# Two branches of one kernel, their steps listed in another order: local attention and a long convolution on one core

## The chip, the core and the metric

The kernel runs on one core of one Trainium2 chip. The core has five engines with a queue each: TensorE (PE in the profile, with its weight loads shown as PEld), VectorE (DVE), ScalarE (ACT), GpSimd (POOL) and SyncE (SP, which here only issues transfers). Sixteen DMA engines move the data. The metric is the time of one execution on the device in microseconds. Smaller is better.

## The reference

Two computations that share nothing stand side by side; their results are concatenated along the last axis. S = 2048 tokens, D = 576 channels, everything in bf16.

```python
def A(x, wqkv, wo):                 # attention in a dilated local window
    q, k, v = split(x @ wqkv)       # 32 heads of 18 channels
    idx  = pos[:, None] - 2 * arange(8)[None, :]       # 8 earlier tokens, every second one
    attn = softmax(where(idx >= 0, q . k[idx] * 18**-0.5, -1e9))
    return (attn @ v[idx]) @ wo

def B(q, k, v, shift_k, ssm_k, ssm_D):                 # long convolution with a gate
    kv = conv4(k, shift_k) * v      # 4 taps along the tokens, channel by channel
    y  = irfft(rfft(kv, 2 * S) * rfft(ssm_k, 2 * S))[:S] + kv * ssm_D
    return q * y

out = concatenate([A(...), B(...)], axis=-1)           # 2048 x 1152
```

The kernel computes the transforms of B as matrix products in two stages, with a trip through DRAM between them, because the second stage needs another split of the data over the partitions.

## The kernel before

Every piece of work is a small Python function, a *step*. One string lists the steps in the order in which they are emitted; a step's arguments stand behind dots. The framework that builds the program then places the instructions of each engine. It starts from this list, and may let instructions of neighbouring steps pass one another, so each engine's final queue is close to the list and not identical to it.

```python
STEP = dict(xt=x_tr, ia=ia_tables, sk=sk_step, qk=qk_step, qt=qk_tail_step, lkv=load_kv, ..., cv=kv_conv,
            sx=x_part, kt=k_tr, kp=k_part, v=v_step, ha=halo, lm=l_mul, lb=l_sum, sa=softmax_a, sb=softmax_b,
            at=at_step, kl=..., xl=..., ks=k_spec, xs=x_spec, gp=g_prod, gi=g_inv, pm=p_mul, ps=p_sum,
            po=p_out, yl=y_load, ys=y_step)
for item in ORDER.split():
    name, *args = item.split(".")
    STEP[name](*map(int, args))
```

What the steps do, and the lines by which the profile names them:

| Step | Work | Engine and line |
|---|---|---|
| xt | transpose x | PE L285, copies DVE L275 and ACT L288 |
| qk, qt | projections of q and k, 512 columns to a matmul | PE L381, L388, copies ACT L382, L390, L391 |
| ia | tables of the inverse transform | PE L401, copies ACT L404 |
| cv | 4 taps and the product with v of B | DVE L446, L451, L452 |
| sx, kp | first stage of the transform of kv and of ssm_k, written to DRAM (Dx, Dk) | PE L417, copies ACT L421, DMA L424 |
| kt | transpose ssm_k | PE L465, copies DVE L275 |
| v, ha | projection of v; the earlier tokens of the next row | PE L368, copies ACT L369; DMA L593 to L596 |
| lm, lb | products q*k, their sums by head | DVE L486, L488; PE L496, L502, copies ACT L505 |
| sa, sb, at | softmax in two parts, transpose of the weights, once for each half (0, 1) | DVE L512 to L517, ACT L518; DVE L524 to L532; PE L540, copies ACT L542 |
| kl, xl, ks, xs | read Dk or Dx back; second stage of the transform | SP L554; PE L549, copies ACT L551; ks also swaps halves by DMA, POOL L560 and L561 |
| gp, gi | product of the spectra; inverse second stage, written to Dy | DVE L568; PE L582, copies ACT L584, DMA L587 |
| pm, ps, po | weights times v; their sum; output projection | DVE L604, L606; PE L618, L626, copies ACT L623, L628; PE L637, copies ACT L639 |
| yl, ys | read Dy and q of B back; last stage, gate, output | SP L647, POOL L648; PE L657, DVE L658 |

The steps of the convolution and the attention compete for buffers. PSUM has two tiles for each of two pools, and nearly all areas in SBUF are handed out to rings of two to four slots. A step that takes a slot waits until the step that held it has ended:

```python
pa = ctx.enter_context(tc.tile_pool(name="pa", bufs=2, space=PS))   # psA: qk, v, lb, ps, po, at
pb = ctx.enter_context(tc.tile_pool(name="pb", bufs=2, space=PS))   # psB: sx, kp, ks, xs, gi, ys
...
tAr = Ring(mc.take(4, D), mc.take(4, D))                 # result of cv, freed by its last sx
prr = Ring(*[mw.take(2, 2, 128, 8) for _ in range(3)])   # products of lm, freed by lb
Kr  = Ring(mk.take(2, 8, HD), mk.take(2, 8, HD))         # spectra of k, freed by the second gp
Xr  = Ring(mx.take(8, HD), mx.take(8, HD))               # spectra of kv, freed by the second gp
Wr  = Ring(mk.take(8, HD), mk.take(8, HD), wx)           # what kl, xl and yl read: three slots
Pp  = Ring(*[mw.take(2, 4, HD) for _ in range(4)])       # products of gp
```

The steps that matter most in the second half:

```python
def k_spec(i):                                        # ks
    Kc = Kr.get(i)
    s2(Wr[("k", i)], i % 4, Kc[:, 0], 1.0 / 2048)     # 8 matmuls L549, 4 copies L551
    Wr.drop(("k", i))
    nc.gpsimd.dma_start(Kc[0:64, 1], Kc[64:128, 0])   # L560
    nc.gpsimd.dma_start(Kc[64:128, 1], Kc[0:64, 0])   # L561

def g_prod(i, hv):                                    # gp
    nc.vector.tensor_tensor(Pp.get((i, hv)), Kr[i][:, :, 4 * hv:4 * hv + 4, :],
                            Xr[i][:, 4 * hv:4 * hv + 4, :]...to_broadcast([128, 2, 4, HD]), ALU.mult)   # L568
    if hv:
        Kr.drop(i)
        Xr.drop(i)

def at_step(hf):                                      # at: needs sb of the same half
    L = Lh[hf].rearrange("p w (a b) -> p w b a", b=2)
    ... 16 transposes L540 ...
```

The index i of ks, xs, gp and gi runs over 8 groups: 0 to 3 for the first half of the channels, 4 to 7 for the second. Reading Dy back for one half of the channels (yl.0 to yl.3, yl.4 to yl.7) needs all four gi of that half.

Of the kernel before, what the change touches and what calls it, by code (L numbers as in the profile page):

```python
# [15 lines left out]


ORDER = """
xt.0 sk qk.0.0.0 qk.1.0.0 qk.0.1.0 qk.1.1.0 ia xt.1 lkv.1 lwv qk.0.0.1 qk.1.0.1 qk.0.1.1 qk.1.1.1 xt.2 xt.3 lkn cv.0
sx.0.0 qk.0.0.2 sx.0.1 sx.0.2 qk.1.0.2 sx.1.0 sx.1.1 sx.1.2 qk.0.1.2 lkv.2 cv.1 qk.1.1.2 sx.2.0 sx.2.1 sx.2.2 qk.0.0.3  # L20
sx.3.0 sx.3.1 qk.1.0.3 sx.3.2 lkv.3 cv.2 qk.0.1.3 sx.4.0 sx.4.1 qk.1.1.3 sx.4.2 sx.5.0 sx.5.1 qt.0 sx.5.2 cv.3 qt.1
sx.6.0 sx.6.1 sx.6.2 qt.2 sx.7.0 sx.7.1 qt.3 sx.7.2 kt.0 lm.0.0 v.0 kp.0.0 lm.0.1 kt.1 lm.0.2 v.1 kp.0.1 lb.0 v.2
kp.0.2 lm.1.0 kp.1.0 lm.1.1 v.3 kt.2 lm.1.2 kp.1.1 lb.1 ha.0 kp.1.2 lm.2.0 v.4 kp.2.0 lm.2.1 kt.3 lm.2.2 v.5 kp.2.1
lb.2 v.6 kp.2.2 lm.3.0 kp.3.0 lm.3.1 v.7 kt.4 lm.3.2 kp.3.1 lb.3 ha.1 kp.3.2 lm.4.0 v.8 kp.4.0 lm.4.1 sa.0 kt.5 lm.4.2
v.9 kp.4.1 lb.4 v.10 kp.4.2 lm.5.0 sb.0 kp.5.0 lm.5.1 v.11 kt.6 lm.5.2 kp.5.1 lb.5 at.0 ha.2 kp.5.2 lm.6.0 v.12 kp.6.0
lm.6.1 kt.7 lm.6.2 v.13 kp.6.1 lb.6 v.14 kp.6.2 lm.7.0 kp.7.0 lm.7.1 v.15 kp.7.1 lm.7.2 kp.7.2 lb.7 ha.3 lwo kl.0 ks.0
xl.0 xs.0 kl.1 ks.1 xl.1 xs.1 pm.0.0 pm.0.1 sa.1 ps.0.0 ps.0.1 gp.0.0 gp.0.1 kl.2 ks.2 xl.2 xs.2 gi.0.0 gi.0.1 gp.1.0
gp.1.1 kl.3 ks.3 xl.3 xs.3 gi.1.0 gi.1.1 pm.1.0 pm.1.1 sb.1 ps.1.0 ps.1.1 gp.2.0 gp.2.1 kl.4 ks.4 xl.4 xs.4 po.0.0
po.0.1 gi.2.0 gi.2.1 pm.2.0 pm.2.1 at.1 ps.2.0 ps.2.1 gp.3.0 gp.3.1 kl.5 ks.5 xl.5 xs.5 po.1.0 po.1.1 gi.3.0 gi.3.1
gp.4.0 gp.4.1 kl.6 ks.6 xl.6 xs.6 gi.4.0 gi.4.1 pm.3.0 pm.3.1 ps.3.0 ps.3.1 gp.5.0 gp.5.1 kl.7 ks.7 xl.7 xs.7 po.2.0  # L30
po.2.1 gi.5.0 gi.5.1 yl.0 ys.0.0 ys.0.1 pm.4.0 pm.4.1 ps.4.0 ps.4.1 gp.6.0 gp.6.1 po.3.0 po.3.1 gi.6.0 gi.6.1 yl.1
ys.1.0 ys.1.1 yl.2 ys.2.0 ys.2.1 pm.5.0 pm.5.1 ps.5.0 ps.5.1 gp.7.0 gp.7.1 po.4.0 po.4.1 gi.7.0 gi.7.1 yl.3 ys.3.0
ys.3.1 pm.6.0 pm.6.1 ps.6.0 ps.6.1 po.5.0 po.5.1 yl.4 ys.4.0 ys.4.1 yl.5 ys.5.0 ys.5.1 pm.7.0 pm.7.1 ps.7.0 ps.7.1
po.6.0 po.6.1 yl.6 ys.6.0 ys.6.1 yl.7 ys.7.0 ys.7.1 po.7.0 po.7.1
"""


# [664 lines left out]
```

## Time and profile before

| | |
|---|---|
| Median of 3 runs | 271.38 us (270.62 to 272.32) |
| Span of the profiled execution | 271.3 us |
| Busy: PE, weight loads, DVE, ACT, POOL | 234.1, 153.0, 191.1, 173.8, 25.2 us |
| Data moved by DMA | 55.24 MB, 204 GB/s over the span |
| Granted TensorE clock, mean | 0.969 of full speed |

The program has three parts, one after the other. To about 75 us it transposes x, projects q and k, and convolves kv. To about 142 us it forms the attention weights, projects v and transforms ssm_k. After that it multiplies spectra, applies the weights to v and writes both outputs. Each line of a timeline gives start, duration, engine, line and operation, the output and the input, the number of instructions merged, and in brackets how long the engine sat idle before and which engine, buffer and line released it. In an answer about stretches, each row has the stretch, then busy microseconds (and instructions) of PE, PEld, DVE, ACT and POOL, then the granted TensorE clock as a share of full speed, the busy share of the DMA engines and what they moved in GB/s. A busy PE is not a PE at its peak: ends of matmuls are modelled and overlap.

### The profile page before, as it was taken

Reading aid. Unit: us, or ns where it says so; the run is one execution under the profiler, and the core shown is the slowest. Engines: PE = TensorE matmul, PEld = TensorE weight load, DVE = VectorE, ACT = ScalarE, POOL = GpSimd, SP = SyncE. Lnnn points to the kernel's source line nnn. Section 1 sums busy time; section 2 is a strip of 40 time slices with the busy share of each in tenths; the row PEclk is TensorE's granted clock in tenths of the full one; section 3 lists DMA queues with packets and bytes.
Section 4 is the critical chain, followed back from the end, with each engine's and each line's share of the span. In section 5 each row is a group of like instructions: output and inputs, shape, how many; then the busy total and the mean of one; then the engine's idle time right before and its main releaser. Section 6 shows DMA issues by size and latency. Waiting matters only on the chain.

```text
span 271.3 us, 5026 instructions
## 1 busy us (share of the span) xinstructions
PE 234.1 (86%) x2013; PEld 153.0 (56%) x2013; DVE 191.1 (70%) x211; ACT 173.8 (64%) x252; POOL 25.2 (9%) x62
## 2 busy tenths in 40 slices
PE   2689998999799999995993978778999998898894
PEld 2225645444357366652752836545877777777682
DVE  1666999967989679999439881579847528965412
ACT  0557958587976566597636398787799974362131
POOL 8600000000000000000201011110211001101000
PEclk9999999999999999997797799997999999999999
DMA  7999851814415435326579789998679999557945
GB/s 248 296 352 364 262 179 22 243 29 146 124 52 174 130 89 152 111 88 190 177 232 249 213 228 256 301 261 270 213 205 305 239 238 303 197 143 225 328 135 174
DMA packets 43758, 55.24 MB, mean 204 GB/s; under 512 B 2284, under 2 KB 36284, under 8 KB 43736
## 3 DMA queue, kind: packets, MB, share of 16 engines
q1 hardware_dynamic: 41766, 47.71, 58.6%
q0 software_dynamic: 1968, 7.23, 10.3%
q8 instruction: 15, 0.25, 0.4%
q14 instruction: 7, 0.06, 0.1%
q10 hardware_dynamic: 2, 0.00, 0.0%
HBM read 29.27 MB, written 18.87 MB: 177 GB/s over the span
## 4 chain that ended last, share of the span: by engine, by line
PE 54%; ACT 18%; DMA 16%; DVE 6%; issue 3%; SPq 1%; POOL 0%; ACTq 0%; DVEq 0%
PE psA L381 13%; PE psA L618 8%; PE psA L368 7%; DMA area<-Dx 7%; ACT area L551 6%; PE psA L502 5%; PE psB L417 4%; DMA area<-area 4%; PE psA L637 3%; ACT area L421 3%; DMA area<-in_A_wqkv_dram 3%; PE psB L582 3%; DMA area<-Dy 3%; PE psB L549 3%; DVE area L604 2%
## 5 line engine op out<-in xcount | busy, mean ns | idle before, releaser
L551 ACT ACTIVATE area<-psB 128x576 bf16<-128x576 f32 x64 | 38.4, 651 | 11.5 <-PE psB L549 11.0
L486 DVE TENSOR_TENSOR area<-area 128x2048 bf16<-128x2048 bf16 x32 | 38.5, 1230 | 7.3 <-PE psA L502 7.2
L421 ACT ACTIVATE area<-psB 128x768 bf16<-128x768 f32 x48 | 37.5, 812 | 7.9 <-PE psB L417 7.4
L618 PE MATMUL psA<-ident,area 128*128 128x128 bf16 x512 | 38.4, 228 | 4.2 <-DVE area L604 3.7
L381 PE MATMUL psA<-area,area 128*128 128x512 bf16 x160 | 40.2, 403 | 1.7 <-ACT area L288 1.7
L604 DVE TENSOR_TENSOR area<-area,area 128x4096 bf16<-128x4096 bf16 x16 | 36.4, 2287 | 4.3 <-PE psA L618 4.1
L618 PEld LDWEIGHTS <-area 128*128 128x128 bf16 x512 | 34.5, 103 | 6.8 <-DVE area L604 4.0
L568 DVE TENSOR_TENSOR area<-area,area 128x2304 bf16<-128x2304 bf16 x16 | 21.1, 1355 | 23.5 <-DMA area<-area 23.5
L549 PE MATMUL psB<-area,W 128*128 128x288 bf16 x128 | 26.3, 293 | 7.3 <-DMA area<-Dx 3.9
L381 PEld LDWEIGHTS <-area 128*128 128x128 bf16 x160 | 16.0, 102 | 23.5 <-issue 8.0
L446 DVE TENSOR_TENSOR area<-area,area 128x2304 bf16<-128x2304 bf16 x16 | 21.6, 1354 | 6.4 <-PE psB L417 4.0
L637 PE MATMUL psA<-wv,area 128*128 128x288 bf16 x160 | 24.5, 291 | 1.6 <-ACT area L623 1.3
L417 PE MATMUL psB<-area,T 128*128 128x384 bf16 x96 | 23.5, 338 | 2.7 <-ACT area L421 2.3
L382 ACT ACTIVATE area<-psA 128x1024 bf16<-128x1024 f32 x16 | 16.4, 1026 | 13.9 <-PE psA L381 13.8
L368 PE MATMUL psA<-wv,area 128*128 128x288 bf16 x160 | 23.8, 295 | 0.0
L368 PEld LDWEIGHTS <-area 128*128 128x128 bf16 x160 | 20.0, 146 | 5.5 <-issue 4.2
L582 PE MATMUL psB<-area,IAt 128*128 128x288 bf16 x128 | 19.6, 286 | 3.1 <-ACT area L584 1.2
L623 ACT ACTIVATE area<-psA 128x1024 bf16<-128x1024 f32 x8 | 8.2, 1023 | 21.5 <-PE psA L618 21.5
L658 DVE TENSOR_TENSOR area<-psB,area 128x576 bf16<-128x576 f32 x16 | 11.6, 754 | 14.2 <-PE psB L657 10.0
L584 ACT ACTIVATE area<-psB 128x576 bf16<-128x576 f32 x32 | 19.6, 654 | 3.0 <-PE psB L582 1.7
L549 PEld LDWEIGHTS <-W 128*128 128x128 bf16 x128 | 12.1, 99 | 16.0 <-issue 8.4
L648 POOL DMA_DIRECT2D area<-in_B_q_dram x8 | 6.1, 768 | 155.3 <-PE psA L540 118.8
(116 smaller groups left out, 298.4 us busy)
## 6 DMA issues: line engine op xcount, KB each, us to landing
Dx<-area SPq DMA_DIRECT2D x16, 288.0 KB, 3.0
Dk<-area SPq DMA_DIRECT2D x16, 288.0 KB, 3.1
area<-Dk SPq DMA_DIRECT2D x8, 576.0 KB, 8.6
area<-Dx SPq DMA_DIRECT2D x8, 576.0 KB, 8.7
area<-area POOLq DMA_DIRECT2D x16, 288.0 KB, 7.9
Dy<-area SPq DMA_DIRECT2D x8, 576.0 KB, 4.2
out_dram<-area SPq DMA_DIRECT2D x16, 288.0 KB, 2.9
area<-Dy SPq DMA_DIRECT2D x8, 576.0 KB, 7.3
```

The costliest lines, as they stand in the source:

```text
L368: nc.tensor.matmul(ps[:, di, 0:288], xTt[:, kb, t2, :], wv[:, kb, d0:d1], start=(kb == 0), stop=(kb == 4))
L381: nc.tensor.matmul(ps[:, u, :], wcols(kb, comp, 2 * cp + u), xT[:, kb, t], start=(kb == 0), stop=(kb == 4))
L417: nc.tensor.matmul(ps[:, ri, 0:384], T1[:, ri, :], sf[:, 384 * ch:384 * ch + 384], start=True, stop=not extra)
L421: nc.scalar.activation(vst[:, :, 384 * ch:384 * ch + 384], ps[:, :, 0:384], ACT.Copy)
L446: nc.vector.tensor_tensor(dst, kfull[:, 4 * c + 3 - j:4 * c + 7 - j, :], skb[:, j, :].unsqueeze(1).to_broadcast([128, 4, D]), ALU.mult)
L486: nc.vector.tensor_tensor(dst[:, u], halves(q2[h], hf), halves(k2[h][:, :, shs[u]:shs[u] + S], hf), ALU.mult)
L549: nc.tensor.matmul(ps[:, hp, 0:HD], W2[:, 8 * g + 2 * prl + hp].rearrange("p i l f -> p (i l f)"), Wt[:, 2 * prl + hp, :], start=True, sto ...
L551: nc.scalar.activation(dst[:, 2 * prl:2 * prl + 2, :], ps[:, :, 0:HD], ACT.Copy, scale=scale)
L582: nc.tensor.matmul(ps[:, hp, 0:HD], IAt[:, zi, 8 * g + hl, :], Pp[(i, hv)][:, zi, hl % 4, :], start=(zi == 0), stop=(zi == 1))
L604: nc.vector.tensor_tensor(P.rearrange("p w (d h) -> p w d h", h=H), vs[:, :, 0:16], at.to_broadcast([128, W, 16, H]), ALU.mult)
L618: nc.tensor.matmul(oaccs[tp][:, u, ct, :], P[:, wi, 128 * ct:128 * ct + 128], ident[:], start=(ct == 0 and wi == 0), stop=(wi == W - 1 and ...
L637: nc.tensor.matmul(ps[:, di, 0:288], lhs, wot[:, ct if ct < 4 else 4 + u, d0:d1], start=(ct == 0), stop=(ct == 4))
```

## The change

Only the string of steps is changed. No step, no buffer and no instruction is added or taken away; each step gets the same arguments as before. The aim is that no engine's queue stands behind an instruction whose input isn't there yet. Steps of the spectra, of the weighting and of the v projection, which stood in regular blocks, are interleaved singly (for example `gp.0.0 gi.0.0 pm.0.1 xl.2 xs.1 gp.0.1 pm.1.0` where before four pm stood ahead of both gp.0).

```diff
 ORDER = """
-xt.0 sk qk.0.0.0 qk.1.0.0 qk.0.1.0 qk.1.1.0 ia xt.1 lkv.1 lwv qk.0.0.1 qk.1.0.1 qk.0.1.1 qk.1.1.1 xt.2 xt.3 lkn cv.0
-sx.0.0 qk.0.0.2 sx.0.1 sx.0.2 qk.1.0.2 sx.1.0 sx.1.1 sx.1.2 qk.0.1.2 lkv.2 cv.1 qk.1.1.2 sx.2.0 sx.2.1 sx.2.2 qk.0.0.3
-sx.3.0 sx.3.1 qk.1.0.3 sx.3.2 lkv.3 cv.2 qk.0.1.3 sx.4.0 sx.4.1 qk.1.1.3 sx.4.2 sx.5.0 sx.5.1 qt.0 sx.5.2 cv.3 qt.1
-sx.6.0 sx.6.1 sx.6.2 qt.2 sx.7.0 sx.7.1 qt.3 sx.7.2 kt.0 lm.0.0 v.0 kp.0.0 lm.0.1 kt.1 lm.0.2 v.1 kp.0.1 lb.0 v.2
-kp.0.2 lm.1.0 kp.1.0 lm.1.1 v.3 kt.2 lm.1.2 kp.1.1 lb.1 ha.0 kp.1.2 lm.2.0 v.4 kp.2.0 lm.2.1 kt.3 lm.2.2 v.5 kp.2.1
-lb.2 v.6 kp.2.2 lm.3.0 kp.3.0 lm.3.1 v.7 kt.4 lm.3.2 kp.3.1 lb.3 ha.1 kp.3.2 lm.4.0 v.8 kp.4.0 lm.4.1 sa.0 kt.5 lm.4.2
-v.9 kp.4.1 lb.4 v.10 kp.4.2 lm.5.0 sb.0 kp.5.0 lm.5.1 v.11 kt.6 lm.5.2 kp.5.1 lb.5 at.0 ha.2 kp.5.2 lm.6.0 v.12 kp.6.0
-lm.6.1 kt.7 lm.6.2 v.13 kp.6.1 lb.6 v.14 kp.6.2 lm.7.0 kp.7.0 lm.7.1 v.15 kp.7.1 lm.7.2 kp.7.2 lb.7 ha.3 lwo kl.0 ks.0
-xl.0 xs.0 kl.1 ks.1 xl.1 xs.1 pm.0.0 pm.0.1 sa.1 ps.0.0 ps.0.1 gp.0.0 gp.0.1 kl.2 ks.2 xl.2 xs.2 gi.0.0 gi.0.1 gp.1.0
-gp.1.1 kl.3 ks.3 xl.3 xs.3 gi.1.0 gi.1.1 pm.1.0 pm.1.1 sb.1 ps.1.0 ps.1.1 gp.2.0 gp.2.1 kl.4 ks.4 xl.4 xs.4 po.0.0
-po.0.1 gi.2.0 gi.2.1 pm.2.0 pm.2.1 at.1 ps.2.0 ps.2.1 gp.3.0 gp.3.1 kl.5 ks.5 xl.5 xs.5 po.1.0 po.1.1 gi.3.0 gi.3.1
-gp.4.0 gp.4.1 kl.6 ks.6 xl.6 xs.6 gi.4.0 gi.4.1 pm.3.0 pm.3.1 ps.3.0 ps.3.1 gp.5.0 gp.5.1 kl.7 ks.7 xl.7 xs.7 po.2.0
-po.2.1 gi.5.0 gi.5.1 yl.0 ys.0.0 ys.0.1 pm.4.0 pm.4.1 ps.4.0 ps.4.1 gp.6.0 gp.6.1 po.3.0 po.3.1 gi.6.0 gi.6.1 yl.1
-ys.1.0 ys.1.1 yl.2 ys.2.0 ys.2.1 pm.5.0 pm.5.1 ps.5.0 ps.5.1 gp.7.0 gp.7.1 po.4.0 po.4.1 gi.7.0 gi.7.1 yl.3 ys.3.0
-ys.3.1 pm.6.0 pm.6.1 ps.6.0 ps.6.1 po.5.0 po.5.1 yl.4 ys.4.0 ys.4.1 yl.5 ys.5.0 ys.5.1 pm.7.0 pm.7.1 ps.7.0 ps.7.1
-po.6.0 po.6.1 yl.6 ys.6.0 ys.6.1 yl.7 ys.7.0 ys.7.1 po.7.0 po.7.1
+xt.0 sk qk.0.0.0 qk.1.0.0 cv.0 qk.1.1.0 qk.0.1.0 lkv.1 xt.1 xt.2 qk.0.1.1 lkv.2 xt.3 ia qk.1.0.1 sx.0.0 lwv sx.0.1
+qk.1.1.1 sx.0.2 sx.1.0 qk.1.0.3 sx.1.1 cv.1 sx.1.2 qk.0.0.1 sx.2.0 cv.2 sx.2.1 sx.2.2 qk.1.0.2 sx.3.0 lkn qt.0
+qk.1.1.2 sx.3.1 qk.0.0.2 sx.3.2 sx.4.0 qk.0.1.2 sx.4.1 qk.0.0.3 sx.4.2 lkv.3 sx.5.0 qt.3 cv.3 sx.5.1 qk.0.1.3 qt.2
+sx.5.2 qt.1 qk.1.1.3 sx.6.0 kt.0 v.1 sx.6.1 v.2 sx.6.2 v.0 sx.7.0 lm.0.0 sx.7.1 kt.1 sx.7.2 kp.0.0 lm.1.0 lm.0.1
+lm.0.2 lb.0 lm.1.1 lm.1.2 kp.0.1 lm.2.0 lb.1 v.3 kp.0.2 kp.1.0 v.4 v.5 lm.3.0 ha.0 lm.2.1 kp.1.1 kt.2 kp.1.2 kp.2.0
+lm.2.2 lb.2 kp.2.1 lm.3.1 lm.3.2 v.7 lb.3 kt.3 kp.2.2 v.6 lm.4.0 kt.4 kp.3.0 kp.3.1 kp.3.2 kp.4.0 sa.0 kp.4.1 kp.4.2
+kt.5 kp.5.0 lm.4.1 sb.0 v.8 lm.4.2 lm.5.0 v.9 lb.4 lm.5.1 v.10 kt.6 kp.5.1 v.11 kp.5.2 lm.5.2 lb.5 kp.6.0 at.0 ha.1
+v.13 kt.7 lm.6.0 v.15 lm.6.1 kp.6.1 v.14 ha.2 kp.6.2 kp.7.0 lm.6.2 lb.6 kp.7.1 v.12 lm.7.0 lm.7.1 lwo lm.7.2 ha.3
+kp.7.2 kl.0 xl.0 lb.7 ks.0 xs.0 kl.1 xl.1 ks.1 sa.1 kl.2 pm.0.0 ps.0.0 gp.0.0 gi.0.0 pm.0.1 xl.2 xs.1 gp.0.1 pm.1.0
+gp.1.0 ps.0.1 ks.2 xl.3 xs.3 gp.1.1 xs.2 gi.0.1 gp.2.0 gi.1.0 xl.4 ps.1.0 gp.2.1 gi.1.1 kl.3 kl.4 gi.2.0 pm.1.1 ks.3
+pm.2.0 ps.1.1 po.0.0 xs.4 ks.4 po.0.1 gp.3.0 xl.5 gi.2.1 pm.2.1 kl.5 ps.2.0 gp.3.1 ks.5 po.1.0 sb.1 pm.3.0 ps.2.1
+gi.3.0 po.1.1 gp.4.0 gp.4.1 at.1 gi.3.1 kl.6 ps.3.0 pm.3.1 xs.5 pm.4.0 po.2.0 gp.5.0 xl.6 gi.4.0 ps.3.1 gp.5.1 gi.4.1
+yl.0 xs.6 ks.6 ys.0.0 xl.7 gi.5.0 po.2.1 ps.4.0 kl.7 ks.7 pm.4.1 po.3.0 xs.7 gp.6.0 ys.0.1 ps.4.1 gi.5.1 yl.1 gi.6.0
+gp.6.1 gp.7.0 po.3.1 pm.5.0 yl.2 ys.1.0 po.4.0 pm.5.1 ys.1.1 gi.6.1 ys.2.0 pm.6.0 ps.5.0 gi.7.0 ps.5.1 gp.7.1 gi.7.1
+yl.3 po.4.1 pm.6.1 ys.2.1 yl.4 ps.6.0 ys.3.0 ys.3.1 po.5.0 po.5.1 pm.7.0 yl.5 ps.6.1 ys.4.0 ys.4.1 po.6.0 ys.5.0 yl.6
+ps.7.0 po.6.1 yl.7 ys.5.1 pm.7.1 ps.7.1 ys.6.0 ys.6.1 po.7.0 ys.7.0 ys.7.1 po.7.1
 """
```

## The prediction, made before the changed kernel ran

> **What bounds the kernel now.** I read the shares of the engines first, then their busy time in eleven stretches that I cut at the seams of the three parts, then the idle notes in the timelines of VectorE and TensorE, and last the totals of the waits.
>
> ```profile
> PE 234.1 (86%) x2013; PEld 153.0 (56%) x2013; DVE 191.1 (70%) x211; ACT 173.8 (64%) x252; POOL 25.2 (9%) x62
> 42.00:75.30 33.30, 30.37 (x165) 14.78 (x164) 28.99 (x27) 26.52 (x36) 0.00 (x0) 1.00 0.43 121
> 116.00:141.80 25.80, 22.48 (x179) 13.28 (x177) 17.57 (x21) 17.25 (x22) 1.52 (x2) 0.87 0.59 174
> 141.80:160.00 18.20, 12.39 (x108) 9.55 (x105) 15.90 (x16) 10.84 (x17) 2.01 (x4) 0.81 0.82 226
> 160.00:186.00 26.00, 20.49 (x173) 14.46 (x171) 15.46 (x13) 20.88 (x37) 3.18 (x7) 0.95 1.01 276
> 204.00:231.00 27.00, 25.21 (x260) 19.98 (x259) 16.67 (x14) 19.99 (x35) 2.85 (x5) 1.00 0.96 271
> ```
>
> No engine is full from end to end. TensorE is nearest, and where it isn't full, another queue stands still too: from 116 to 142 us VectorE works 17.57 of 25.8 us, and from 160 to 186 us the DMA engines are full (share 1.01) while TensorE idles 5.5 us. So it is a chain that changes hands, and an order can help exactly where a queue stood behind something late. These are the places:
>
> ```profile
> 62.72 1.36 DVE L446 TENSOR_TENSOR area<-area,area 128x2304 bf16<-128x2304 bf16 x1 [4.03 <-PE psB L417]
> 127.62 1.22 DVE L532 TENSOR_TENSOR area<-area 128x2048 bf16<-128x2048 bf16 x1
> 135.94 2.38 DVE L486 TENSOR_TENSOR area<-area 128x2048 bf16<-128x2048 bf16 x2 [4.13 <-PE psA L502]
> 142.50 0.17 DVE L512 TENSOR_TENSOR area<-area,maskb 128x16 bf16<-128x16 bf16 x1 [4.18 <-ACT area L505]
> ```
> ```profile
> 128.90 1.89 PE L540 MATMUL psA<-ident,area 128*128 128x128 bf16 x16 [0.54 <-DVE area L532]
> 147.71 5.92 PE L618 MATMUL psA<-ident,area 128*128 128x128 bf16 x59 [3.69 <-DVE area L604]
> 191.80 1.05 PE L540 MATMUL psA<-ident,area 128*128 128x128 bf16 x16
> ```
> ```profile
> DVE area L568 <- DMA area<-area: 23.5, 6, 5.9
> ```
>
> The first is the last convolution (cv.3), which waits for the slot that the first-stage matmuls of cv.1 hold. The next ones are one knot: softmax b of half 0 ends late on VectorE (L532, 127.6 us), the transposes L540 stand in TensorE's queue for it, the head sums behind them come late, and VectorE then lacks the slot of its next product (4.13 us), and later the last sum (4.18 us). The last is the product of spectra, which waits 23.5 us in all for the swap of halves.
>
> **What the Trainium skill says.** "PSUM — Partial Sum Buffer", section "Engine vs sequencer instructions", says that matmuls start and complete in program order and that the queues of VectorE and ScalarE are strictly first in, first out. The trace agrees: nothing of PE passes L540 at 128.90. "TensorE: Matmul & The Clock Gate", section "HAM oscillation — how this bites in real kernels", says that idle gaps of over about 3.4 us let the array fall back to half clock. Here the 16 transposes L540 take 1.89 us at 128.9 us and 1.05 us at 191.8 us, and the granted clock reads 0.50 from 126 to 132 us, after a stretch in which PE was busy only 0.83 and 1.04 us of two times 2 us. The single gaps there are under 1 us, so here a thin stretch did it too. After the 3.69 us gap it is 0.50 again until about 152 us. "DMA: Bandwidth & Descriptors", section "Issuing engines are not separate DMA queues", says that transfers of all issuing engines interleave on the same 16. The trace agrees: a swap of 288 KB takes 7.9 us in the median beside reads of 576 KB that take 8.6 us. "Perfetto Trace Analysis", section "Optimization Strategy", recommends interleaving regimes with different busiest engines, which is what this change does; no run shown yet says whether it pays here.
>
> **The change part by part.** Removed and added: nothing. The built order of instructions shows the same matmuls, copies and transfers on every engine; only places differ. So the gain is idle time taken away, less idle time that is new.
>
> *Part one (to 75.3 us).* On PE the tables stretch from 25.1 to 34.0 us has 128 matmuls L401 (16 of them take 0.57 us, so 4.6), 20 transposes (1.3) and 9 matmuls L381 at 0.216 (1.9): 7.8 of 8.9 us. From 40.8 to 47.4 us it has 40 transposes (2.5) and 12 matmuls L417 (0.65 for 4, so 1.9): 4.4 of 6.6 us. From 68.1 to 75.3 us it has 20 matmuls L388 (4.3) and 8 L417 (1.3), 5.6 of 7.2 us, held by the small copies L390 and L391. Together 4.9 us are lost. The new order puts all 60 remaining transposes into the tables stretch, where ScalarE's copies (about 0.95 us each) are the limit, and spreads the four qt among qk. I take 3 of the 4.9 us as regained on PE. On DVE the first three convolutions run back to back in both orders and end at about 57.5 to 58 us. In the new order the 24th L417, the last that reads cv.1's result, stands behind about 120 of the 160 L381. Counting from about 39 us, where the tables end, that is 60 L381 (13.0), 5 L388 (1.1) and 24 L417 (3.9): about 57 us, so the slot is free at 58 us and the 4.03 us go. PE and DVE then enter part two both about 4 us earlier; these overlap and count once: **4 us**.
>
> *Part two (to 141.8 us).* The place of L540 among PE's matmuls is the same: 40 L368, 2 L417 and two head sums follow it in both. But on DVE 25 products L486 and 12 L488 stand ahead of L532 instead of 28 and 14. That is 3 x 1.23 + 2 x 0.4 = 4.5 us less ahead of it. L532 ended at 128.8; with 8.5 us less (4 + 4.5) PE should no longer be late for it, the thin stretch before it mostly fills, and the 4.13 us of DVE go. DVE has its 4.5 us of work later instead, which just fills the hole at 131.8. The sum of what DVE has to do up to lb.7 is unchanged, so its two waits are the measure: 4.03 + 4.13. I count the second as **4 us**, with the half clock of 126 to 132 us already inside it.
>
> *The seam (141.8 to 160 us).* Sum L505 (0.6), five softmax instructions (2.9), product L604 (2.3), then ps: this chain of 5.8 us is the same in both. PE has 12 L549 ahead of the first L618 instead of 8; the added four wait for Dx.0, which SyncE can issue only behind ha.3 and lwo (144.1 us before, 8.7 us to land). PE thus waits for data up to 5 us more, with L618 behind it, but the second spectrum of k comes sooner. DVE has gp.0.0 after 2 products L604 instead of 4, and will wait for the swap about 6 us instead of 1.46. Both engines have room here; I count **1 us lost**.
>
> *Part three.* It needs 16 reads (9.4 MB), swaps (4.7), Dy out and back (9.4), q (2.4) and results (4.7): 30.6 MB, of which the 276 GB/s of the full stretch would take 111 us. From 137 us, when Dk.0 is read, to the end are 134 us. DMA is therefore close behind, and a better order can't win much. In favour: softmax b and at of half 1 come later relative to gp, so gp.4 to gp.5 (191.4 to 204.7 us, 13.3 us against 10 on the average) may close up by 2 us. Against: xl.3 and xl.4 are read ahead of kl.3, whose path with the swap is longer, and xs.2 now waits for gp.1.1. I count **0**. In the tail, after gp.7.1, DVE has 3 L604 and 14 L658 left instead of 4 and 14; PE's remaining work after the last gi is about 27 us instead of 24. It doesn't matter while PE is full.
>
> Sum: 4 + 4 - 1 + 0 = 7 us. 271.4 - 7 = 264.4 us.
>
> **The rivals.** *DMA takes it all back.* If part three is paced by transfers (share 0.96 to 1.01 in 160 to 186 and 204 to 231 us), starting it 8 us earlier helps only as far as its reads start earlier. For it: those rows. Against: DMA share is 0.72 from 186 to 204 and 0.56 from 231 to 245 us, so it has holes. It would make 267 to 270 us. *New waits in strict queues.* Finely mixed lists mean that one late swap or read holds everything behind it: gp.0.0 early on DVE, xs.0 ahead of ps on PE, xs.3 ahead of xs.2. For it: 23.5 us of L568 waiting already. Against: these engines have idle time in that stretch. It would make 272 to 278 us. *TensorE warm throughout.* If the fuller queue keeps the clock up in both cold stretches, about 5 us more are saved and 258 us is possible. Against: the seam's gap remains.
>
> **Range and chances.** The centre is 264.4. Only the parts before the seam rest on counted waits; part three carries an error of about 5 us either way. 8 in 10: 257.5 to 270.5 us. The 2% limit is 265.95 us, 1.5 us above the centre, so faster by over 2% gets 0.60, within 2% 0.31, slower 0.09.
>
> **What would show it.** Right: no wait of about 4 us on L446 or L486 in the new timeline of DVE; L540 of half 0 near 120 us with about 1 us for 16; L512 of half 1 at 133 to 136 us instead of 142.5. Seam: a PE gap ahead of xs.0 and a DVE wait of about 6 us ahead of the first L568. Part three: from L512 of half 1 to the end 128 to 131 us, as the 128.8 us before. The prediction is wrong if this last stretch is longer or shorter by over 5 us, or if L512 comes after 138 us.

## The result and the profile after

The changed order takes 264.13 us (median of 4 runs, 262.06 to 267.53) against 271.19 us; the ratio is 0.971, with a 95% interval of 0.964 to 0.978. Medians here are of all executions, while ratios leave out those that took over 1.5% longer than the quickest of the same kernel, so the two can differ. When the same kernel ran again beside its variants, it took 263.98 us, ratio 0.973 (0.969 to 0.978). The prediction was 264.4 us. The profile shown here is of that second time; its span is 262.6 us.

The first view is the line of busy shares of the engines. Then come stretches of the second and third part, cut at the new seam (columns as in the rows of stretches shown before):

```profile
PE 226.1 (86%) x2007; PEld 151.6 (58%) x2013; DVE 190.6 (73%) x211; ACT 173.1 (66%) x252; POOL 25.1 (10%) x62
```
```profile
42.00:75.30 33.30, 32.97 (x175) 17.43 (x177) 32.88 (x30) 28.43 (x38) 0.00 (x0) 1.00 0.43 125
116.00:134.60 18.60, 16.22 (x148) 9.37 (x141) 13.76 (x17) 10.96 (x17) 1.51 (x2) 1.00 0.75 214
134.60:160.00 25.40, 16.85 (x167) 12.42 (x167) 19.66 (x18) 18.29 (x30) 3.12 (x6) 0.87 0.88 247
160.00:186.00 26.00, 22.78 (x206) 17.52 (x204) 19.07 (x19) 20.40 (x35) 3.08 (x6) 0.93 0.84 260
204.00:231.00 27.00, 20.42 (x195) 15.50 (x192) 14.40 (x14) 14.04 (x24) 3.65 (x6) 0.94 0.83 223
```

From 42 to 75.3 us VectorE now works 32.88 of 33.3 us (28.99 before): its wait for the slot of cv.1 is gone. TensorE's clock is full in the two stretches ahead of the seam. But from 204 to 231 us TensorE works only 20.42 us, where it had 25.21 (and 20.91 us from 196 to 223 us, the same stretch moved forward by the 8 us gained): part three has lost something there that it had before. The timelines show both sides, VectorE first and then TensorE:

```profile
119.46 1.22 DVE L532 TENSOR_TENSOR area<-area 128x2048 bf16<-128x2048 bf16 x1
...
129.30 2.38 DVE L486 TENSOR_TENSOR area<-area 128x2048 bf16<-128x2048 bf16 x2 [1.53 <-PE psA L502]
...
134.60 0.17 DVE L512 TENSOR_TENSOR area<-area,maskb 128x16 bf16<-128x16 bf16 x1 [2.92 <-ACT area L505]
...
139.91 2.29 DVE L604 TENSOR_TENSOR area<-area,area 128x4096 bf16<-128x4096 bf16 x1 [2.37 <-DMA area<-area]
...
147.97 1.36 DVE L568 TENSOR_TENSOR area<-area,area 128x2304 bf16<-128x2304 bf16 x1 [3.24 <-DMA area<-area]
```
```profile
121.80 1.05 PE L540 MATMUL psA<-ident,area 128*128 128x128 bf16 x16
...
141.02 1.14 PE L549 MATMUL psB<-area,W 128*128 128x288 bf16 x4 [4.91 <-DMA area<-Dx]
...
223.64 1.14 PE L657 MATMUL psB<-area,IB 128*128 128x288 bf16 x4 [4.62 <-DMA area<-Dy]
```

The last softmax (L512 of half 1) begins at 134.60 us instead of 142.50: 7.9 us earlier. From there to the end it takes 128.0 us, against 128.8 before. In these two profiles the whole gain is thus made ahead of the seam. At the seam TensorE waits 4.91 us for Dx, as was expected; at 223.64 us it waits 4.62 us for Dy, which was not.

The profile of the kernel before is of an execution that took 273.77 us, 2.4 us over its median. A difference of one or two microseconds between parts is therefore read from the medians of the variants below and not from these two profiles.

### The profile page after: what moved, and what is told of

It is laid out like the page before. It is cut to its first block, busy times and chain, and to the rows that moved or that the text cites. A ratio compares the mean times of both kernels' runs of the same rounds, so it can differ in the third digit from the quotient of the medians.

```text
span 265.8 us, 4987 instructions
## 1 busy us (share of the span) xinstructions
PE 228.5 (86%) x2013; PEld 153.0 (58%) x2013; DVE 190.5 (72%) x211; ACT 173.2 (65%) x252; POOL 25.2 (9%) x62
## 4 chain that ended last, share of the span: by engine, by line
PE 57%; DMA 24%; ACT 12%; issue 2%; SPq 2%; DVE 1%; POOL 0%; ACTq 0%; DVEq 0%; POOLq 0%
PE psA L381 13%; DMA area<-area 7%; DMA area<-Dy 7%; PE psA L368 7%; PE psA L618 7%; PE psB L417 5%; PE psA L502 5%; PE psA L637 5%; PE psB L549 4%; PE psB L657 3%; DMA area<-in_A_wqkv_dram 3%; PE psB L582 3%; ACT area L421 2%; DMA area<-Dk 2%; DMA Dy<-area 2%
## 5 line engine op out<-in xcount | busy, mean ns | idle before, releaser
L486 DVE TENSOR_TENSOR area<-area 128x2048 bf16<-128x2048 bf16 x32 | 37.9, 1225 | 4.7 <-PE psA L502 4.7
L618 PE MATMUL psA<-ident,area 128*128 128x128 bf16 x512 | 40.2, 227 | 0.2 <-ACT area L623 0.2
L618 PEld LDWEIGHTS <-area 128*128 128x128 bf16 x512 | 35.2, 102 | 4.4 <-DVE area L604 0.6
L549 PE MATMUL psB<-area,W 128*128 128x288 bf16 x128 | 27.0, 301 | 10.8 <-DMA area<-Dx 4.8
L568 DVE TENSOR_TENSOR area<-area,area 128x2304 bf16<-128x2304 bf16 x16 | 21.2, 1355 | 16.2 <-DMA area<-area 15.0
L637 PE MATMUL psA<-wv,area 128*128 128x288 bf16 x160 | 26.2, 296 | 0.1
L639 ACT ACTIVATE area<-psA 128x576 bf16<-128x576 f32 x16 | 10.4, 652 | 23.8 <-PE psA L637 19.6
L417 PE MATMUL psB<-area,T 128*128 128x384 bf16 x96 | 22.2, 327 | 1.8 <-ACT area L421 1.6
L368 PE MATMUL psA<-wv,area 128*128 128x288 bf16 x160 | 23.0, 288 | 0.7 <-ACT area L542 0.7
L446 DVE TENSOR_TENSOR area<-area,area 128x2304 bf16<-128x2304 bf16 x16 | 21.5, 1353 | 2.4 <-ACT area L439 2.2
L368 PEld LDWEIGHTS <-area 128*128 128x128 bf16 x160 | 20.0, 145 | 5.0 <-issue 4.1
L382 ACT ACTIVATE area<-psA 128x1024 bf16<-128x1024 f32 x16 | 16.4, 1023 | 9.8 <-PE psA L381 9.7
L549 PEld LDWEIGHTS <-W 128*128 128x128 bf16 x128 | 12.2, 101 | 18.0 <-issue 8.0
```

The source lines that it names most:

```text
L368: nc.tensor.matmul(ps[:, di, 0:288], xTt[:, kb, t2, :], wv[:, kb, d0:d1], start=(kb == 0), stop=(kb == 4))
L417: nc.tensor.matmul(ps[:, ri, 0:384], T1[:, ri, :], sf[:, 384 * ch:384 * ch + 384], start=True, stop=not extra)
L446: nc.vector.tensor_tensor(dst, kfull[:, 4 * c + 3 - j:4 * c + 7 - j, :], skb[:, j, :].unsqueeze(1).to_broadcast([128, 4, D]), ALU.mult)
L486: nc.vector.tensor_tensor(dst[:, u], halves(q2[h], hf), halves(k2[h][:, :, shs[u]:shs[u] + S], hf), ALU.mult)
L549: nc.tensor.matmul(ps[:, hp, 0:HD], W2[:, 8 * g + 2 * prl + hp].rearrange("p i l f -> p (i l f)"), Wt[:, 2 * prl + hp, :], start=True, sto ...
L618: nc.tensor.matmul(oaccs[tp][:, u, ct, :], P[:, wi, 128 * ct:128 * ct + 128], ident[:], start=(ct == 0 and wi == 0), stop=(wi == W - 1 and ...
```

## The experiments

**Which part carries the gain.** Three hybrids take one part of the list from each kernel.

```diff
 h_front:  part one, up to the last sx         -before +after     parts two and three as before
 h_12:     parts one and two, up to kl.0       -before +after     part three as before
 h_3:      part three, from kl.0 on            -before +after     parts one and two as before
```

> Part one (up to the last sx) listed as in the changed kernel, all the rest as before. Theory (two separate waits of VectorE were removed, about 4 us each, and what is gained before the seam is kept to the end): about 267.5 us; no 4 us wait on L446, L512 of half 1 at about 138.5 us instead of 142.5. Rival 1 (part three is paced by DMA and takes gains back): 269.5 to 271 us although L512 comes earlier. Rival 2 (the second wait of VectorE grows by what the first gives): L512 stays at 141 to 142.5 us and the time at 271.

> Parts one and two listed as in the changed kernel, everything from the first read of the spectra on as before. Theory (the whole gain is made before the seam, part three is worth nothing): 263 to 265.5 us, L512 of half 1 at about 135 us, and from there to the end about 129 us. Rival (the interleaved part three carries a share of the gain): 267 to 269 us.

> Parts one and two as before, everything from the first read of the spectra on as in the changed kernel. Theory: 270 to 273 us, L512 of half 1 still at 142 to 143 us, and a PE wait of about 5 us for Dx ahead of the weighting. Rival (part three carries a share): 265 to 268 us.

| | Median, us | Ratio to before (95%) | L512 of half 1, us | From there to the end, us |
|---|---|---|---|---|
| before | 271.0 beside these | | 142.50 | 128.8 |
| h_front | 266.57 | 0.986 (0.977 to 0.995) | 138.25 | 126.7 |
| h_12 | 264.99 | 0.980 (0.973 to 0.987) | 134.77 | 127.2 |
| h_3 | 275.18 | 1.017 (1.011 to 1.022) | 143.27 | 128.7 |

Part one brings L512 forward by 4.25 us and part two by another 3.5 us, and from there to the end the profiles show 126.7 and 127.2 us, so in them neither is given back. In the medians part one is worth 4.5 us (3.8 us by the ratio), but part two only 1.6 us more; with intervals this wide, the rest of its 3.5 us is neither shown nor excluded at the end. The rival that part three is paced by DMA and takes gains back, which put h_front at 269.5 to 271 us, falls. h_12 alone reaches the time of the whole change within the intervals. VectorE's timeline of h_front shows why the second step is separate:

```profile
131.73 2.38 DVE L486 TENSOR_TENSOR area<-area 128x2048 bf16<-128x2048 bf16 x2 [3.94 <-PE psA L502]
...
138.25 0.17 DVE L512 TENSOR_TENSOR area<-area,maskb 128x16 bf16<-128x16 bf16 x1 [4.14 <-ACT area L505]
```

Everything has come 4.2 us earlier, and the second wait is still there in full (3.94 us against 4.13). It goes only with part two (1.51 us in h_12).

h_3 was expected at 270 to 273 us and took 275.18: alone, the new part three costs 4 us. The wait of about 5 us for Dx, expected ahead of the weighting, is not in its trace; TensorE waits there for the first product, as in the kernel before:

```profile
148.56 6.26 PE L618 MATMUL psA<-ident,area 128*128 128x128 bf16 x59 [3.78 <-DVE area L604]
...
232.96 1.14 PE L657 MATMUL psB<-area,IB 128*128 128x288 bf16 x4 [5.09 <-DMA area<-Dy]
```

The order at the seam goes with the list of part two and not with that of part three: ahead of the first L618, TensorE has 8 matmuls L549 in the kernel before, in h_front and in h_3, and 12 in h_12 and in the changed kernel. Further on, h_3 has a wait of 5.09 us for Dy, like the one of the changed kernel, which a test below finds to cost 4.0 us. Behind the new front the new part three costs nothing that can be told (0.973 against 0.980, intervals overlapping). Why it is worse behind the old front wasn't settled.

**The knot of part two.** In the kernel before, only the transposes of half 0 are moved.

```diff
-... kp.5.1 lb.5 at.0 ha.2 ... kp.6.1 lb.6 v.14 ...
+... kp.5.1 lb.5 ha.2 ... kp.6.1 lb.6 at.0 v.14 ...
```

> The kernel before with the transposes of the softmax weights of half 0 (at.0) listed only after the seventh head sum; the weight products of half 0 then stand differently at the seam too. Theory of the knot (the transposes stand in TensorE's queue for softmax b, and everything behind them is late): the 4.13 us wait of VectorE on L486 falls under 2 us, the half clock at 126 to 132 us shortens or goes, and L512 of half 1 comes at 138 to 140 us; the time 268 to 271 us, as the seam is changed too. Rival (VectorE's own order, not the transposes, makes the wait): L512 stays at 142 us or later, the time at 271 or more.

Measured: 273.58 us, ratio 1.011 (1.006 to 1.017), while L512 of half 1 comes at 138.31 us, 4.2 us earlier. VectorE and then TensorE in that kernel:

```profile
129.15 4.67 DVE L486 TENSOR_TENSOR area<-area 128x2048 bf16<-128x2048 bf16 x4
...
138.31 0.17 DVE L512 TENSOR_TENSOR area<-area,maskb 128x16 bf16<-128x16 bf16 x1 [3.79 <-ACT area L505]
```
```profile
122.15 1.39 PE L368 MATMUL psA<-wv,area 128*128 128x288 bf16 x10
...
130.78 1.07 PE L540 MATMUL psA<-ident,area 128*128 128x128 bf16 x16
...
145.57 4.66 PE L618 MATMUL psA<-ident,area 128*128 128x128 bf16 x42 [7.93 <-DVE area L604]
```

The knot is what it was taken for: with the transposes out of the way the wait on L486 is gone, and the 16 transposes take 1.07 us at full clock instead of 1.89. In the kernel before, the idle note on L540 is only 0.54 us long. What the move sets free are the v projections L368 listed behind it: two of them now run ahead of L540, the first at 122.15 us, and from 122 to 126 us TensorE is busy 3.95 us instead of 1.87. The half clock is not what makes the wait: in h_3, where the first two parts are those of the kernel before, the clock stayed full until 130 us and the transposes took 1.10 us, and VectorE waited 4.14 us on L486 all the same.

The time doesn't follow, because the built order turned at the seam: the weightings L618 now stand ahead of all spectra L549, TensorE waits 7.93 us for the first product of the weighting, and the first product of spectra comes at 164.61 us instead of 156.72. From L512 to the end it takes 134.2 us instead of 128.8. The time was expected at 268 to 271 us; this second effect was foreseen and put too low.

**The changed kernel again, and its wait for Dy.** Here three of the last-stage steps are moved behind work that doesn't wait.

> The changed kernel once more, unaltered, beside its variants. Expected 262 to 265 us; in the profile 126 to 129 us from L512 of half 1 to the end, which would say that part three of the changed list is worth within 1 us of the old one's (126.7 and 127.2 us behind the new front).

```diff
-... yl.2 ys.1.0 po.4.0 pm.5.1 ys.1.1 gi.6.1 ys.2.0 pm.6.0 ps.5.0 gi.7.0 ps.5.1 gp.7.1 gi.7.1 yl.3 ...
+... yl.2 po.4.0 pm.5.1 gi.6.1 pm.6.0 ps.5.0 ys.1.0 gi.7.0 ys.1.1 ps.5.1 gp.7.1 gi.7.1 ys.2.0 yl.3 ...
```

> The changed list with ys.1.0, ys.1.1 and ys.2.0 moved some steps later, so that TensorE has the sums ps.5 and inverse steps gi.7 ahead of the matmuls that wait for Dy. Theory (the 5.9 us PE wait for Dy, with the half clock behind it, is a new wait in a strict queue and costs what it lasts): 258.5 to 261 us, the wait under 2 us. Rival (the last groups of the convolution set the end whatever PE does in between): the wait goes and the time stays within 1 us of the changed kernel.

The changed kernel took 263.98 us and after_ys 259.97 us, ratio to before 0.958 (0.954 to 0.962): 4.0 us less, which is nearly the wait itself. In the timeline of TensorE the matmuls that had waited now stand behind sums and inverse steps, and find their data there:

```profile
223.61 0.65 PE L657 MATMUL psB<-area,IB 128*128 128x288 bf16 x4
...
227.96 0.65 PE L657 MATMUL psB<-area,IB 128*128 128x288 bf16 x4
```

No idle note stands behind these, and four matmuls take 0.65 us; after its wait the same group took 1.14 us. The rival, that TensorE's wait doesn't matter there, falls.

**The transposes of half 1.** Behind the new front, and with part three listed as before (h_12), TensorE stands for softmax b of half 1 at at.1.

```diff
-... pm.2.0 pm.2.1 at.1 ps.2.0 ps.2.1 gp.3.0 ... gi.3.0 gi.3.1 gp.4.0 ...
+... pm.2.0 pm.2.1 ps.2.0 ps.2.1 gp.3.0 ... gi.3.0 gi.3.1 at.1 gp.4.0 ...
```

> Parts one and two of the changed list, part three of the old one, with at.1 moved behind gi.3 so that TensorE doesn't stand for softmax b of half 1. Theory (the 2.33 us PE wait ahead of L540 and the half clock around 180 us cost about 3 us): 261 to 263 us. Rival (part three is paced by the transfers of the spectra there): 264 to 265.5 us, as without the move.

> The kernel before with one step moved: at.1, the transposes of half 1, from ahead of ps.2 to behind gi.3. Theory (the place of at.1 in TensorE's queue alone cost the old part three 5 to 6 us, as behind the new front): 264.5 to 267 us, L512 of half 1 unmoved at 142.5 us, gp.4 to gp.5 about 10 us instead of 13. Rival (it only paid because the new front shifts part three against the transfers): 269 to 271 us.

Behind the new front (h12_at1) the time is 259.18 us, ratio 0.956 (0.952 to 0.960), which is 5.8 us less than h_12 by the medians and 6.6 us by the ratios. About 3 us had been expected. TensorE in h_12, then the same sums L618 in the kernel before, then two stretches of h_12 (150 us to its last matmul, and 178 to 186 us), then the corresponding long stretch of h12_at1:

```profile
180.13 1.89 PE L540 MATMUL psA<-ident,area 128*128 128x128 bf16 x16 [2.33 <-DVE area L532]
181.81 5.67 PE L618 MATMUL psA<-ident,area 128*128 128x128 bf16 x64
```
```profile
192.69 3.74 PE L618 MATMUL psA<-ident,area 128*128 128x128 bf16 x64
```
```profile
150.00:258.70 108.70, 98.14 (x1000) 77.93 (x997) 70.54 (x65) 68.60 (x115) 10.79 (x18) 0.97 0.84 236
178.00:186.00 8.00, 5.87 (x57) 5.87 (x58) 5.16 (x6) 2.43 (x3) 1.55 (x2) 0.57 0.71 231
```
```profile
150.00:252.00 102.00, 95.66 (x1003) 75.34 (x1000) 70.78 (x65) 68.09 (x115) 10.83 (x18) 1.00 0.88 251
```

The wait itself is 2.33 us. What makes it dear is the clock, which is 0.57 of full speed over these eight microseconds and 0.50 from 180 to 184 us: the transposes take 1.89 us instead of 1.05, and the 64 sums behind them 5.67 us instead of 3.74. Wait and slower work add up to 5.1 us, most of what the move brings. With at.1 moved, these sums run ahead of it and the clock is full from 150 us on. The products of spectra close up behind it: gp.4 to gp.5 takes 15.4 us in h_12 and 9.8 us in h12_at1 (L568 at 180.89 and 196.34 us, against 179.99 and 189.79).

In the kernel before (b_at1) the same move gives 269.37 us, ratio 0.988 (0.982 to 0.994): a gain of 2.2 us by the medians and 3.2 us by the ratio, and not of 5 to 6, so the theory's size is wrong there and the rival, which expected 269 to 271 us, holds in part. The kernel before shows why the large gain couldn't come: its transposes of half 1 have no idle note and take 1.05 us (the line at 191.80 us in the prediction). TensorE reaches them only after softmax b has ended at 191.45 us, so it never stood there. In h_12 TensorE has finished what comes ahead of them at 177.80 us, and softmax b ends at 180.08 us. What the smaller gain of b_at1 consists of was not settled; its gp.4 to gp.5 takes 10.8 us instead of 13.3, in an execution 3.0 us over its median.

**Reads of k ahead of reads of kv.**

```diff
-... ks.2 xl.3 xs.3 gp.1.1 xs.2 gi.0.1 ... gi.1.1 kl.3 kl.4 gi.2.0 pm.1.1 ks.3 pm.2.0 ...
+... ks.2 kl.3 xl.3 xs.3 gp.1.1 ks.3 xs.2 gi.0.1 ... gi.1.1 kl.4 gi.2.0 pm.1.1 pm.2.0 ...
```

> The changed list with kl.3 ahead of xl.3 and ks.3 ahead of xs.2. Theory of the prediction's third part (reads of kv ahead of those of k make the longer path late): gp.3 comes 41 us after L512 of half 1 or sooner instead of 45, and the time falls by 1 to 3 us. Rival (gp isn't on the path there, later groups wait for other slots): gp.3 earlier, the time unchanged within 1 us.

Measured: ratio 0.980 (0.975 to 0.986) against 0.973 (0.969 to 0.978) for the changed kernel, which is about 2 us slower, with intervals that overlap. (The medians, 268.07 and 263.98 us, lie 4 us apart.) gp.3 does come earlier, 40.3 us after L512 of half 1 instead of 45.3. But gp.4 then comes at 58.3 us instead of 51.0. VectorE in this kernel at that place:

```profile
175.93 2.63 DVE L568 TENSOR_TENSOR area<-area,area 128x2304 bf16<-128x2304 bf16 x2 [0.31 <-DMA area<-area]
...
193.91 2.63 DVE L568 TENSOR_TENSOR area<-area,area 128x2304 bf16<-128x2304 bf16 x2 [7.80 <-DMA area<-area]
```

The wait, 4.44 us ahead of gp.3 in the changed kernel, was moved to the next group and grew to 7.80 us. The gain of 1 to 3 us is refuted. The end hardly feels that gp.4 is 7 us later: in the profiles it takes 127.6 us from L512 to the end against 128.0. That speaks for the rival, that gp isn't on the path there, though a small loss isn't excluded.

**The seam.** Taking h12_at1, the loads of the output weights are listed later, so that the reads of Dk and Dx no longer stand behind them in SyncE's queue.

```diff
-... lm.7.1 lwo lm.7.2 ha.3 kp.7.2 lb.7 kl.0 ks.0 xl.0 xs.0 kl.1 ks.1 xl.1 xs.1 ...
+... lm.7.1 lm.7.2 ha.3 kp.7.2 lb.7 kl.0 ks.0 xl.0 xs.0 kl.1 ks.1 xl.1 lwo xs.1 ...
```

> The variant with the new front, the old part three and at.1 late, with lwo listed behind xl.1, so that the first reads of Dk and Dx no longer stand behind the loads of wo and the halo in SyncE's queue. In the built order the first products of spectra then stand ahead of all weightings on VectorE. Theory of strict queues (the wait for the swap now holds the weightings too): the 4.7 us PE wait for Dx goes or halves, but the first L604 comes 8 to 12 us later and the time rises to 261 to 265 us. Rival (the seam's PE wait and its half clock are what is left to win): 255 to 258 us.

Measured: 271.84 us, slower than h12_at1 by 12.7 us in the medians and 11.8 us in the ratios, and level with the kernel before (0.999, 0.996 to 1.003). VectorE and TensorE in u2:

```profile
148.88 2.63 DVE L568 TENSOR_TENSOR area<-area,area 128x2304 bf16<-128x2304 bf16 x2 [10.67 <-DMA area<-area]
151.42 2.28 DVE L604 TENSOR_TENSOR area<-area,area 128x4096 bf16<-128x4096 bf16 x1
```
```profile
137.41 0.66 PE L549 MATMUL psB<-area,W 128*128 128x288 bf16 x4 [0.64 <-DMA area<-Dx]
...
153.76 0.40 PE L618 MATMUL psA<-ident,area 128*128 128x128 bf16 x2 [12.12 <-DVE area L604]
```

The wait for Dx has fallen to 0.64 us, as meant. But in the built order the pair gp.0 now stands ahead of the weightings on VectorE, waits 10.67 us for the swap with them behind it, and TensorE waits 12.12 us. The direction was expected, the size (261 to 265 us) wasn't. Whether the seam's wait can be taken out without turning that order was not tried to an end. The edit moved nothing but the loads; VectorE's order turned all the same, since the framework may let neighbouring steps pass one another.

The lowest time measured is that of h12_at1, 259.18 us: the new parts one and two, the old part three, and at.1 behind gi.3. after_ys (0.958, 0.954 to 0.962) can't be told from it.

## Why the prediction was right, and where it was not

*Part one, 4 us.* Right. h_front moved L512 by 4.25 us and the median by 4.5 (3.8 by the ratio). The wait of 4.03 us on L446 is gone. The prediction let TensorE and VectorE each gain about 4 us here and counted them once; which of the two sets the gain wasn't tried alone.

*Part two, 4 us.* Right in mechanism, and in size at the seam: L512 comes 3.5 us earlier from h_front to h_12, and 4.2 us when only the transposes are moved. At the end the medians show 1.6 us between h_front and h_12. The half clock from 126 to 132 us went with it, though h_3 shows that the wait doesn't depend on it; the trace now has 1.00 in those stretches. L540 came at 121.8 us instead of "near 120". That three products fewer ahead of L532 do this, rather than the rest of the new list of part two, wasn't tried alone.

*The seam, 1 us lost.* Right within what can be told: h_front keeps the old seam and takes 126.7 us from L512 to the end, h_12 has the new one and takes 127.2. TensorE's 4.91 us wait is as foreseen. VectorE's wait for the swap is 3.24 us and not 6, because the halo held the first weighting back for 2.37 us first, which the step had left out.

*Part three, 0 us.* The sum is right and the reason isn't, so that the total came within half a microsecond is in part luck. The gp.4 to gp.5 gap did close by 2.4 us (from 13.3 to 10.9 us, L568 at 185.62 and 196.51). Against it stands a wait that the prediction didn't name: TensorE's 4.62 us for Dy, which costs 4.0 us. A second one, 2.04 us for a copy at 182.01 us with the clock at 0.53 behind it, was not taken up. The sentence that the tail doesn't matter while PE is full took for granted that PE is full. The step that failed outright is "DMA is therefore close behind, and a better order can't win much". Moving one step, at.1, made the stretch from L512 to the end 120.5 us instead of 127.2, and the DMA share from 150 us on is 0.88 instead of 0.84. (Of these 6.8 us, the medians show 5.8: the profiled execution of h12_at1 took 257.45 us, 1.7 us under its median.) The 111 us of transfers were an estimate from the rate of one stretch, and the old part three stood 16 us above it. And "reads of kv ahead of k" was counted as a loss; turning them round brought nothing.

*The rivals.* DMA taking the gain back is refuted by h_front for part one, and h12_at1 and after_ys show that part three had room. New waits in strict queues came true in part three; in sum they cost about what the closed gaps gave. TensorE warm throughout didn't come: the clock is 0.50 from 138 to 144 us and again after the wait for Dy.

## What to carry to other kernels

Where a counted wait lies ahead of everything that follows, an order's gain can be read from the idle notes: here two waits of about 4 us each came back as 4.25 and 3.5 us at the seam. In strictly ordered queues one instruction whose input is late can hold up ready work behind it. Look for it in TensorE's queue (transposes that wait for a softmax, a last stage that waits for DRAM), in the trace of the very kernel that is to be changed, and move that one step before reshuffling a whole list: that brought 5.8 and 4.0 us here, but little where the trace showed no wait (b_at1). Judge the built order of each engine and not the list: an edit on one queue can turn the order on another, and that cost 12 us in u2 and the gain of at0_late.

## What the runs showed of the hardware

A wait of TensorE can cost more than its length. Sixteen transposes take 1.05 to 1.07 us at full clock and 1.89 us at half clock; after a wait of 2.33 us in h_12 the clock was 0.57 over 8 us, and after the 4.91 us wait at the seam 0.50 until 144 us. Taking the wait of 2.33 us away brought 5.8 us. It need not: taking away the wait for Dy, 4.62 us with the clock at 0.50 from 224 to 226 us, brought 4.0 us.

How soon the clock falls in a thin stretch varies. In the kernel before it was 0.50 from 126 us, after TensorE had been busy 0.83 and 1.04 us in the two times 2 us from 122 us on. In h_3, with the same matmuls in that stretch, it was 1.00 until 130 us, with TensorE busy 0.97, 1.19, 0.81 and 0.81 us.
